# Loading only k of the first chunk by a hardware queue, q by GpSimd ahead of all, with a new order of loads and steps, in an attention-then-feed-forward kernel

## The chip, the cores and the metric

The kernel runs on one core of one Trainium2 chip. The metric is the device time of one execution in microseconds (us). The granted clock of the kernel before was 0.999 or 1.0.

## The reference, cut to what matters

```python
# q, k, v: 8 batches x 8 heads x 576 positions x 64, f32
def _attn_ref(q, k, v):                      # sliding window of 64, causal
    scores = scale * np.matmul(q, k.transpose(0, 1, 3, 2))
    mask = (rel >= 0) & (rel < 64)
    ...                                      # softmax over the window
    return np.matmul(attn, v)

def _moe_ref(x, w_gate, w_val, w_out):       # x: 4608 x 512, d_ff 1536
    g = x @ w_gate
    silu = g * (1.0 / (1.0 + np.exp(-g)))
    return silu * (x @ w_val) @ w_out
```

The 4608 tokens are worked in 36 chunks of 128. A chunk is a tile of 128 partitions by 8 heads x 64. Four chunks make one block of 512 columns for the feed-forward.

## The kernel before: what the change touches

Two lists of names make up the opening: LOADS is the order in which loads are issued, STEPS the order in which work is given to the engines. A small dependency tracker puts the waits in.

```python
    LOADS = """
    f:0:1 init kq:1 kq:2 v:0 kq:3 v:1 v:2 v:3 w:7:9 kq:5 kq:4 ... w:10:12
    """
    STEPS = """
    warm:50 ld:8 wo:0:6 B:0 ca:0:0 cd:0:1 W:4 T:0:1 T:0:0 ea:0:1 ed:0:0 TQ:1 qa:1 W:1 S:0 TK:1 ld:9 kd:1 W:1
    TQ:2 qa:2 S:1 B:2 TK:2 kd:2 A0:0 A1:0 M:1 S:2 TQ:3 N:0 B:3 TK:3 qa:3 kd:3 W:1 X:0 A0:1 xa:0 S:3 A1:1 ld:10
    A0:2 N:1 A1:2 ld:11 W:1 A0:3 N:2 A1:3 X:1 xa:1 N:3 W:1 X:2 xa:2 W:1 X:3 F:0:7:0:384 xd:3 U F:0:8 U TK:5
    TQ:5 ka:5 TQ:4 F:0:7:384:512 TK:4 ld:12 qa:4 qd:5 ka:4 U W:2 F:0:3 U S:4 S:5 F:0:6 ...
    """
```

How to read the steps: `warm:50` is 50 matmuls on zeros, `W` filler matmuls on zeros, `B` a mask product (it adds the mask to the scores' bank on TensorE), `ca`/`cd` a cast of half of chunk 0 on ScalarE or VectorE, `T` its transposes, `TQ`/`TK` the transposes of q or k of a later chunk, `qa qd ka kd` the copies of those out of PSUM (a on ScalarE, d on VectorE), `S` scores, `M` the mask on VectorE where there is no `B`, `A0`/`A1` the two halves of attention times v, `N` the normalization on VectorE, `X` the transposes of the result, `xa`/`xd` their copies, `F:c:f:t0:t1` a block of the feed-forward (weight f, columns t0 to t1), `U` its work on VectorE, `O` the last matrix product. In LOADS, `f` is chunk 0's load, `kq:n` q and k of chunk n, `v:n` its v, `w:a:b` a pair of loads of both weights.

Chunk 0's q and k come as f32 on two hardware queues and are cast; every other load comes on GpSimd's queue and is bf16 when it lands: in the trace of before, k of chunk 0 by a hardware queue is 256 KB (`ff`), a q or k chunk by GpSimd 128 KB, with no cast instruction ahead of its transposes.

```python
    def first_load(self, n, own):            # k by SP to partitions 0-63, q by ACT to 64-127
        for eng, p0, src in (("sp", 0, self.k), ("act" if own else "sp", 64, self.q)):
            ...
                a = src[b, :, s:s + L, :].rearrange("h (p j) d -> p h (j d)", j=2)
                self.g.op(eng, lambda e, d=d, a=a: e.dma_start(d, a), writes=[("ff", n, p0 + r)], dma=True)

    def init(self):
        ...                                  # identity and mask on VectorE
        dve(lambda e: e.memset(self.wz[:, 128:512], 0.0), [], ["wz2"])
        ones = self.vall[:, :].rearrange("p (i h d) -> p i h d", i=self.NV, h=H)[:, :, :, 64:80]
        dve(lambda e: e.memset(ones, 1.0), [], [("va", i) for i in range(self.NV)])
```

The column of ones beside v (only column 64 of 64 to 79 is read) makes the matmul give the softmax's sum.

The softmax here doesn't subtract the row's maximum and nothing guards it: scores larger than these inputs give would overflow.

## Time and profile before

| | before |
|---|---|
| time, median of the first 3 runs | 332.33 us (331.69 to 332.67) |
| span of the profiled run | 330.4 us |
| TensorE busy | 98% |
| first scores | 8.42 us |
| first product with v | 10.85 us |
| first normalization on VectorE | 11.97 us |
| first feed-forward matmul | 18.11 us |
| first matmul of the output product O | 71.76 us |

The instructions of the kernel before in order of time show these points. The columns are start in us, duration in us, engine (PE is TensorE, PEld its weight loads, DVE VectorE, ACT ScalarE, POOL GpSimd), line, operation, output and input, shapes, count, and in brackets the idle time before it with what ended it.

```profile
5.98 0.91 DVE L302 CAST cc<-ff 128x512 bf16<-128x512 f32 x1
...
8.42 0.45 PE L423 MATMUL ps<-qT,kT 64*64 64x128 bf16 x24 [0.41 <-DVE qT L302]
...
10.85 0.70 PE L473 MATMUL ps<-va,pt 64*64 64x65 bf16 x24
```

Read it as the path from the cast (L302) through the scores (L423) to attention times v (L473): the scores wait for a copy on VectorE.

### The profile page before, as it was taken

Reading aid. Unit: us, or ns where it says so; the run is one execution under the profiler, and the core shown is the slowest. Engines: PE = TensorE matmul, PEld = TensorE weight load, DVE = VectorE, ACT = ScalarE, POOL = GpSimd, SP = SyncE. Lnnn points to the kernel's source line nnn. Section 1 sums busy time; section 2 is a strip of 40 time slices with the busy share of each in tenths; the row PEclk is TensorE's granted clock in tenths of the full one; section 3 lists DMA queues with packets and bytes.
Section 4 is the critical chain, followed back from the end, with each engine's and each line's share of the span. In section 5 each row is a group of like instructions: output and inputs, shape, how many; then the busy total and the mean of one; then the engine's idle time right before and its main releaser. Section 6 shows DMA issues by size and latency. Waiting matters only on the chain.

```text
span 330.4 us, 8381 instructions
## 1 busy us (share of the span) xinstructions
PE 323.7 (98%) x3544; PEld 165.3 (50%) x3544; DVE 217.1 (66%) x454; ACT 137.2 (42%) x249; POOL 115.6 (35%) x144
## 2 busy tenths in 40 slices
PE   6999999999999999999999999999999999999996
PEld 4655665564455454544445454545454544444444
DVE  7569999993467858485757676767676766555520
ACT  3755466453344344343525252525343432332222
POOL 8999999965017606060706060100000000000000
DMA  9999999999999999999999999542425111100012
GB/s 133 169 170 168 165 179 155 178 139 177 197 166 173 126 148 98 158 97 160 81 177 74 182 72 163 90 111 42 122 29 131 34 63 34 63 34 32 32 65 96
DMA packets 168837, 38.70 MB, mean 117 GB/s; under 512 B 159328, under 2 KB 164320, under 8 KB 168800
## 3 DMA queue, kind: packets, MB, share of 16 engines
q0 software_dynamic: 122560, 18.62, 81.6%
q1 hardware_dynamic: 45568, 19.21, 29.6%
q8 instruction: 28, 0.46, 0.5%
q10 hardware_dynamic: 672, 0.33, 0.4%
q14 instruction: 9, 0.07, 0.1%
HBM read 37.75 MB, written 9.44 MB: 143 GB/s over the span
## 4 chain that ended last, share of the span: by engine, by line
PE 95%; DVE 4%; issue 0%; ACT 0%
PE ps L604 57%; PE ps L637 28%; PE ps L423 3%; PE ps L536 2%; PE ps L310 2%; PE ps L473 1%; DVE xb L495 1%; PE ps L667 1%; PE ps L570 1%; DVE kT L302 0%; DVE va L273 0%; DVE cc L302 0%; DVE rc L492 0%; DVE mask L267 0%; DVE pt L439 0%
## 5 line engine op out<-in xcount | busy, mean ns | idle before, releaser
L613 DVE SCALAR_TENSOR_TENSOR uu<-sig,ps 128x512 bf16<-128x512 bf16 (+3 forms) x116 | 75.1, 647 | 67.1 <-ACT sig L610 66.9
L604 PE MATMUL ps<-xT,Wg 128*128 128x512 bf16 (+3 forms) x464 | 112.3, 365 | 0.0
L604 PE MATMUL ps<-xT,Wv 128*128 128x512 bf16 (+3 forms) x464 | 112.3, 364 | 0.0
L610 ACT ACTIVATE sig<-ps 128x512 bf16<-128x512 f32 (+3 forms) x116 | 65.8, 569 | 87.5 <-PE ps L604 87.4
L637 PE MATMUL ps<-Wo,hT 128*128 128x512 bf16 x420 | 98.0, 379 | 0.2 <-issue 0.2
L615 DVE SCALAR_TENSOR_TENSOR hT<-uu,ps 128x512 bf16<-128x512 bf16 (+3 forms) x116 | 75.4, 650 | 4.0
L373 POOL DMA_DIRECT2D va<-in_v_dram x40 | 40.4, 1036 | 90.0 <-PE ps L536 87.6
L604 PEld LDWEIGHTS ps<-xT,Wv 128*128 128x128 bf16 x464 | 44.7, 98 | 49.0 <-DVE hT L615 0.3
L604 PEld LDWEIGHTS ps<-xT,Wg 128*128 128x128 bf16 x464 | 43.7, 98 | 46.1 <-DMA xT<-xb 0.3
L637 PEld LDWEIGHTS ps<-Wo,hT 128*128 128x128 bf16 x420 | 39.9, 98 | 46.9 <-issue 0.4
L649 ACT ACTIVATE ost<-ps 128x512 f32<-128x512 f32 x35 | 20.9, 597 | 66.5 <-PE ps L637 66.3
L433 ACT ACTIVATE pt<-ps 128x512 bf16<-128x512 f32 x72 | 37.7, 602 | 25.8 <-PE ps L423 25.8
L283 POOL DMA_DIRECT2D kn<-in_k_dram x39 | 40.0, 1048 | 1.6 <-DMA kn<-in_k_dram 1.6
L283 POOL DMA_DIRECT2D qn<-in_q_dram x39 | 39.9, 1042 | 1.9 <-issue 1.1
L439 DVE TENSOR_TENSOR pt<-pt,mask 128x512 bf16<-128x512 bf16 x66 | 24.3, 417 | 0.3
L558 DVE TENSOR_TENSOR xb<-ps,rp 128x448 bf16<-128x448 f32 (+1 forms) x36 | 18.5, 514 | 1.2
L555 DVE RECIPROCAL rp<-ps 128x7 f32<-128x7 f32 (+1 forms) x36 | 6.7, 187 | 15.5 <-PE ps L536 15.5
L423 PE MATMUL ps<-qT,kT 64*64 64x64 bf16 (+1 forms) x864 | 15.8, 203 | 0.6 <-DVE qT L302 0.4
L423 PEld LDWEIGHTS ps<-qT,kT 64*64 64x64 bf16 x864 | 12.3, 108 | 7.2 <-DVE hT L615 4.2
L536 PE MATMUL ps<-va,pt 64*64 64x65 bf16 x728 | 11.5, 193 | 0.1
L495 DVE TENSOR_TENSOR xb<-ps,rc 128x256 bf16<-128x256 f32 x24 | 10.2, 424 | 0.8
L379 POOL DMA_DIRECT2D Wg<-in_moe_w_gate_dram x10 | 9.8, 977 | 0.0
(51 smaller groups left out, 107.4 us busy)
## 6 DMA issues: line engine op xcount, KB each, us to landing
out_dram<-ost SPq DMA_DIRECT2D x35, 256.0 KB, 2.8
va<-in_v_dram POOLq DMA_DIRECT2D x32, 128.0 KB, 6.3
qn<-in_q_dram POOLq DMA_DIRECT2D x31, 128.0 KB, 7.0
kn<-in_k_dram POOLq DMA_DIRECT2D x31, 128.0 KB, 7.0
Wo<-in_moe_w_out_dram POOLq DMA_DIRECT2D x2, 768.0 KB, 11.4
Wg<-in_moe_w_gate_dram POOLq DMA_DIRECT2D x8, 128.0 KB, 5.0
Wv<-in_moe_w_val_dram POOLq DMA_DIRECT2D x8, 128.0 KB, 5.1
Wg<-in_moe_w_gate_dram POOLq DMA_DIRECT2D x2, 256.0 KB, 5.8
```

The lines of the kernel that those rows point to most:

```text
L283: self.g.op("pool", lambda e, d=d, a=a: e.dma_start(d, a), writes=ks, dma=True)
L373: g.op("pool", lambda e, d=d, a=a: e.dma_start(d, a), writes=ks, dma=True)
L423: r = e.matmul(sv[h][o:o + 64, c, q0:q1], self.kT[ps, c, kk:kk + 64], qT[ps, c, q0:q1], start=not biased, stop=not biased or c == 3 and kk ...
L433: g.op("act", lambda e, po=po, si=si: e.activation(po, si, ACTF.Exp, scale=SCALE), reads=[bk], writes=[pk])
L439: "dve", lambda e: e.tensor_tensor(po, po, m, ALU.mult), reads=[pk, "mask"], writes=[pk]))
L558: g.op("dve", lambda e, xo=xo, rb=rb, a=a: e.tensor_tensor(xo, a[:, :, 0:64], rb, ALU.mult), reads=[bk] + rk, writes=wk)
L604: r = e.matmul(bank[:, 0:n], W[:, kk, f * 128:f * 128 + 128], xT[:, kk, t0:t1], start=(kk == 0), stop=(kk == NK - 1))
L610: g.op("act", lambda e: e.activation(sig[:, 0:n], G[:, 0:n], ACTF.Tanh, scale=0.5), reads=[gk], writes=[("sig", i)])
L613: g.op("dve", lambda e: e.scalar_tensor_tensor(uu[:, 0:n], sig[:, 0:n], 1.0, G[:, 0:n], ALU.add, ALU.mult), reads=[("sig", i), gk], writes ...
L615: g.op("dve", lambda e: e.scalar_tensor_tensor(hT[:, f, t0:t1], uu[:, 0:n], 0.5, V[:, 0:n], ALU.mult, ALU.mult), reads=[("uu", i), vk], wr ...
L637: r = e.matmul(OB[:, :], hT[:, f, 128 * u:128 * u + 128], self.Wo[:, f, :], start=(f == 0), stop=(f == NF - 1))
L649: g.op("act", lambda e: e.activation(ost[:, :], OB[:, :], ACTF.Copy), reads=[ok], writes=[("ost", io)])
```

## The change

The intent is to shorten the path of chunk 0: half the bytes on the hardware queue, half the cast, and a smaller memset ahead of it. The two lists are new almost throughout. The diff, cut to its core:

```diff
     LOADS = """
-    f:0:1 init kq:1 kq:2 v:0 kq:3 v:1 v:2 v:3 w:7:9 kq:5 kq:4 ...
+    f:0 init q:0 kq:1 kq:2 v:1 v:0 kq:3 v:2 v:3 w:7:9 w:1:2 w:5:6 kq:4 kq:5 ...
     STEPS = """
-    warm:50 ld:8 wo:0:6 B:0 ca:0:0 cd:0:1 W:4 T:0:1 T:0:0 ea:0:1 ed:0:0 TQ:1 qa:1 W:1 S:0 ...
-    ... A0:0 A1:0 M:1 S:2 TQ:3 N:0 ... W:2 F:0:3 U S:4 S:5 F:0:6 ...
+    warm:45:64 B:0 B:1 ca:0:0 cd:0:1 T:0:1 T:0:0 ea:0:1 TQ:0 ld:8 wo:0:6 ed:0:0 qa:0 W:1 TQ:1 S:0 ...
+    ... A0:0 A0:1 A1:0 A1:1 ld:10 N:0 TQ:3 B:3 qa:3 N:1 TK:3 X:0 ka:3 xa:0 M:2 W:1 S:3 X:1 A0:2 ...
+    ... W:1 X:2 F:0:7:0:256 xd:2 U X:3 F:0:8:0:384 ... S:4 U F:0:3 kd:5 M:4 S:5 U F:0:4 ...
...
-        self.wz = sb("wz", 512)
+        self.wz = sb("wz", 128)            # fillers now read it through a broadcast
...
-        dve(lambda e: e.memset(self.wz[:, 128:512], 0.0), [], ["wz2"])
-        ones = ...[:, :, :, 64:80]
+        ones = ...[:, :, :, 64:66]
...
-    def first_load(self, n, own):
-        for eng, p0, src in (("sp", 0, self.k), ("act" if own else "sp", 64, self.q)):
+    def first_load(self, n):               # k alone, heads 0-3 and 4-7 on the partition halves
+        for u in range(2):
+            d = self.ff[n][64 * u:64 * u + 64].rearrange("p h j d -> p h (j d)")
+            a = self.k[b, 4 * u:4 * u + 4, s:s + L, :].rearrange("h (p j) d -> p h (j d)", j=2)
+            self.g.op("sp", lambda e, d=d, a=a: e.dma_start(d, a), writes=[("ff", n, u)], dma=True)
```

More of the change, by code (lines that the diff above doesn't have):

```diff
@@ L162 @@
     LOADS = """
-    f:0:1 init kq:1 kq:2 v:0 kq:3 v:1 v:2 v:3 w:7:9 kq:5 kq:4 w:3:4 w:6:7 w:4:5 v:5 w:1:2 v:4 w:9:10 w:2:3 v:6
-    w:5:6 v:7 kq:6 w:0:1 kq:7 w:10:12
+    f:0 init q:0 kq:1 kq:2 v:1 v:0 kq:3 v:2 v:3 w:7:9 w:1:2 w:5:6 kq:4 kq:5 w:3:4 w:4:5 w:6:7 v:5 w:2:3 v:6
+    v:4 w:9:10 w:0:1 kq:6 v:7 kq:7 w:10:12
     """
     STEPS = """
-    warm:50 ld:8 wo:0:6 B:0 ca:0:0 cd:0:1 W:4 T:0:1 T:0:0 ea:0:1 ed:0:0 TQ:1 qa:1 W:1 S:0 TK:1 ld:9 kd:1 W:1
-    TQ:2 qa:2 S:1 B:2 TK:2 kd:2 A0:0 A1:0 M:1 S:2 TQ:3 N:0 B:3 TK:3 qa:3 kd:3 W:1 X:0 A0:1 xa:0 S:3 A1:1 ld:10
@@ L169 @@
-    A0:2 N:1 A1:2 ld:11 W:1 A0:3 N:2 A1:3 X:1 xa:1 N:3 W:1 X:2 xa:2 W:1 X:3 F:0:7:0:384 xd:3 U F:0:8 U TK:5
-    TQ:5 ka:5 TQ:4 F:0:7:384:512 TK:4 ld:12 qa:4 qd:5 ka:4 U W:2 F:0:3 U S:4 S:5 F:0:6 M:4 F:0:4 M:5 U F:0:1 U
-    U A0:4 A0:5 A1:4 ld:13 wo:6:12 A1:5 F:0:9 N:4 N:5 X:4 F:0:2 U xa:4 X:5 U F:0:5 xd:5 F:1:1:0:128 U TQ:6
-    F:1:2:0:256 U TK:6 ld:14 qa:6 F:1:3:0:256 U F:0:0 kd:6 U U S:6 TK:7 TQ:7 F:1:0:0:256 kd:7 F:0:10 M:6 U
-    qa:7 U A0:6 S:7 A1:6 ld:15 TQ:8 TK:8 N:6 F:0:11 M:7 ka:8 qd:8 X:6 A0:7 xa:6 U S:8 A1:7 ld:16 F:1:4:0:384
@@ L174 @@
-    N:7 F:1:5:0:384 U X:7 U TQ:9 xa:7 F:1:6:0:384 M:8 qa:9 TK:9 U F:1:7 kd:9 TD:10 U A0:8 S:9 A1:8 ld:17 F:1:8
-    N:8 M:9 X:8 TQ:11 xa:8 F:1:9 U qd:11 A0:9 TK:11 U A1:9 ka:11 F:1:10 N:9 TK:12 U X:9 ka:12 TQ:12 F:1:11
-    xd:9 qd:12 TD:13 S:10 U S:12 F:1:1:128:512 M:10 F:1:0:256:512 M:12 A0:10 U S:11 A1:10 U F:1:2:256:512
-    F:1:3:256:512 N:10 F:1:4:384:512 U XD:10 F:1:5:384:512 O:0:0 U U U M:11 O:0:1 A0:11 S:13 A1:11 O:0:2 N:11
-    M:13 X:11 O:0:3 xd:11 F:1:6:384:512 U TD:14 TD:15
+    warm:45:64 B:0 B:1 ca:0:0 cd:0:1 T:0:1 T:0:0 ea:0:1 TQ:0 ld:8 wo:0:6 ed:0:0 qa:0 W:1 TQ:1 S:0 qd:1 TK:1
@@ new lines @@
+    ld:9 kd:1 W:1 TQ:2 S:1 qd:2 TK:2 kd:2 W:2 S:2 W:1 A0:0 A0:1 A1:0 A1:1 ld:10 N:0 TQ:3 B:3 qa:3 N:1 TK:3 X:0
+    ka:3 xa:0 M:2 W:1 S:3 X:1 A0:2 xd:1 A1:2 ld:11 N:2 W:1 A0:3 A1:3 N:3 W:1 X:2 F:0:7:0:256 xd:2 U X:3
+    F:0:8:0:384 xd:3 F:0:1 U U F:0:5 U TK:4 TQ:4 ld:12 ka:4 TQ:5 F:0:7:256:512 qd:4 TK:5 qa:5 F:0:8:384:512 U
+    S:4 U F:0:3 kd:5 M:4 S:5 U F:0:4 M:5 U F:0:6 U F:0:2 U A0:4 A0:5 A1:4 ld:13 wo:6:12 A1:5 F:0:9 N:4 N:5 X:4
+    F:0:0 U xa:4 X:5 U TK:6 xa:5 TQ:6 ld:14 F:1:0:0:128 ka:6 U F:1:1:0:256 qa:6 TQ:7 U F:1:2:0:256 qd:7 S:6
@@ new lines @@
+    TK:7 U F:1:3:0:256 kd:7 F:0:10 M:6 U U A0:6 S:7 A1:6 ld:15 TQ:8 TK:8 N:6 F:0:11 M:7 ka:8 qd:8 X:6 A0:7
+    xa:6 S:8 U A1:7 ld:16 F:1:4:0:384 N:7 F:1:5:0:384 U X:7 U TQ:9 xa:7 F:1:6:0:384 M:8 qa:9 TK:9 U F:1:7 kd:9
+    TD:10 U A0:8 S:9 A1:8 ld:17 F:1:8 N:8 M:9 X:8 TQ:11 xa:8 F:1:9 U qd:11 A0:9 TK:11 U A1:9 ka:11 F:1:10 N:9
+    TK:12 U X:9 ka:12 TQ:12 F:1:11 xd:9 qd:12 TD:13 S:10 U S:12 F:1:0:128:512 M:10 F:1:1:256:512 M:12 A0:10 U
+    S:11 A1:10 U F:1:2:256:512 F:1:3:256:512 N:10 F:1:4:384:512 U XD:10 F:1:5:384:512 O:0:0 U U U M:11 O:0:1
@@ L179 @@
+    A0:11 S:13 A1:11 O:0:2 N:11 M:13 X:11 O:0:3 xd:11 F:1:6:384:512 U TD:14 TD:15
     """
@@ L209, in alloc @@
         self.qT = [self.qa[:, :, r, :] for r in range(self.NZ)]
-        pairs = lambda t: t[:, :].rearrange("p (h j d) -> p h j d", h=H, j=2)
-        self.ff = [pairs(t) for t in ring("ff", self.NI, H * 128, F32)]
-        self.cc = [t[:, :].rearrange("p (j h d) -> p j h d", j=2, h=H) for t in ring("cc", self.NI, H * 128)]
+        pairs = lambda t: t[:, :].rearrange("p (h j d) -> p h j d", h=H // 2, j=2)
+        self.ff = [pairs(t) for t in ring("ff", self.NI, H * 64, F32)]
+        self.cc = [t[:, :].rearrange("p (j h d) -> p j h d", j=2, h=H // 2) for t in ring("cc", self.NI, H * 64)]
         self.one, self.fi, self.df = [sb(x, 128, F32) for x in ("one", "fi", "df")]
@@ L270, in init, with load_qk @@
         dve(lambda e: e.memset(self.kT[:, :, 0:64], 0.0), [], [("kT", -1, j) for j in range(2)])
-        dve(lambda e: e.memset(self.wz[:, 128:512], 0.0), [], ["wz2"])
-        ones = self.vall[:, :].rearrange("p (i h d) -> p i h d", i=self.NV, h=H)[:, :, :, 64:80]
+        ones = self.vall[:, :].rearrange("p (i h d) -> p i h d", i=self.NV, h=H)[:, :, :, 64:66]
         dve(lambda e: e.memset(ones, 1.0), [], [("va", i) for i in range(self.NV)])
-    def load_qk(self, n):
+    def load_qk(self, n, which="qk"):
         i = n % self.NQ
-        for dst, src, nm in ((self.qn[i], self.q, "qn"), (self.kn[i], self.k, "kn")):
+        for w in which:
+            dst, src, nm = (self.qn[i], self.q, "qn") if w == "q" else (self.kn[i], self.k, "kn")
             parts = list(self.segs(128 * n, 128))
@@ L283, in load_qk @@
                 self.g.op("pool", lambda e, d=d, a=a: e.dma_start(d, a), writes=ks, dma=True)
-    def first_load(self, n, own):
-        for eng, p0, src in (("sp", 0, self.k), ("act" if own else "sp", 64, self.q)):
-            parts = list(self.segs(128 * n, 128))
-            for r, b, s, L in parts:
-                d = self.ff[n][p0 + r // 2:p0 + (r + L) // 2].rearrange("p h j d -> p h (j d)")
-                a = src[b, :, s:s + L, :].rearrange("h (p j) d -> p h (j d)", j=2)
-                self.g.op(eng, lambda e, d=d, a=a: e.dma_start(d, a), writes=[("ff", n, p0 + r)], dma=True)
+    def first_load(self, n):
+        (_, b, s, L), = self.segs(128 * n, 128)
+        for u in range(2):
+            d = self.ff[n][64 * u:64 * u + 64].rearrange("p h j d -> p h (j d)")
+            a = self.k[b, 4 * u:4 * u + 4, s:s + L, :].rearrange("h (p j) d -> p h (j d)", j=2)
+            self.g.op("sp", lambda e, d=d, a=a: e.dma_start(d, a), writes=[("ff", n, u)], dma=True)
     def cast(self, n, half, eng):
-        hs = slice(4 * half, 4 * half + 4)
+        hs = slice(2 * half, 2 * half + 2)
         d = self.cc[n][:, :, hs].rearrange("p j h d -> p h j d")
-        self.move(eng, d, self.ff[n][:, hs], [("ff", n, p) for p in (0, 64)], [("cc", n, half)])
+        self.move(eng, d, self.ff[n][:, hs], [("ff", n, u) for u in (0, 1)], [("cc", n, half)])
     def move(self, eng, d, a, rk, wk):
@@ L316, in first_T @@
     def first_T(self, n, half):
-        job = [self.cc[n][:, j, 2 * c:2 * c + 2, :] for c in (2 * half, 2 * half + 1) for j in range(2)]
+        job = [self.cc[n][:, j, 2 * half:2 * half + 2, :] for j in range(2)]
         self.transposes(("f", n, half), job, [("cc", n, half)])
@@ L321, in first_ev @@
         tb, bk = self.tb["f", n, half]
-        cs = slice(2 * half, 2 * half + 2)
-        ta = tb.rearrange("p (c j) (w t) -> p w c t j", j=2, w=2)
-        kd, qd = self.kT[:, cs, 64 + 128 * n:192 + 128 * n], self.qT[n][:, cs]
-        for w, (d, key) in enumerate(((kd, ("kT", n, half)), (qd, ("qT", n, half)))):
-            self.move(eng, d.rearrange("p c (t j) -> p c t j", j=2), ta[:, w], [bk], [key])
+        d = self.kT[:, half:4:2, 64 + 128 * n:192 + 128 * n].rearrange("p u (t j) -> p u t j", j=2)
+        self.move(eng, d, tb[:, 0:2].rearrange("p j (u t) -> p u t j", u=2), [bk], [("kT", n, half)])
         self.done(bk)
@@ L341, in ev, with warm @@
         self.done(bk)
-    def warm(self, count):
+    def warm(self, count, cols):
         bank, bk = self.ps[7], ("ps", 7)
+        a = self.wz[:, 0:128].unsqueeze(1).to_broadcast([128, cols // 128, 128]) if cols > 128 else self.wz[:, 0:cols]
         def pe(e):
             for _ in range(count):
-                r = e.matmul(bank[:, 0:64], self.wz[:, 0:128], self.wz[:, 0:64], start=True, stop=True)
+                r = e.matmul(bank[:, 0:cols], self.wz[:, 0:128], a, start=True, stop=True)
             return r
@@ L353, in fill @@
     def fill(self, count):
+        a = self.wz[:, :].unsqueeze(1).to_broadcast([128, 4, 128])
         j = min(self.pool, key=lambda i: self.pool[i])
@@ L358, in pe @@
             for _ in range(count):
-                r = e.matmul(bank[:, :], self.wz[:, 0:128], self.wz[:, :], start=True, stop=True)
+                r = e.matmul(bank[:, :], self.wz[:, :], a, start=True, stop=True)
             return r
-        self.g.op("pe", pe, reads=["wz", "wz2"], writes=[bk])
+        self.g.op("pe", pe, reads=["wz"], writes=[bk])
     def load_v(self, n):
@@ L685, in build @@
         acts = {
-            "f": self.first_load, "init": self.init, "v": self.load_v, "w": W, "kq": self.load_qk,
+            "f": self.first_load, "init": self.init, "v": self.load_v, "w": W, "kq": self.load_qk, "q": lambda n: self.load_qk(n, "q"), "k": lambda n: self.load_qk(n, "k"),
             "wo": self.load_wo, "ld": load,
```

## The prediction

> **What bounds the kernel now.** I read the page first: the busy rows, the slices, the chain that ended last.
>
> ```profile
> PE 323.7 (98%) x3544; PEld 165.3 (50%) x3544; DVE 217.1 (66%) x454; ACT 137.2 (42%) x249; POOL 115.6 (35%) x144
> ...
> PE   6999999999999999999999999999999999999996
> ...
> PE 95%; DVE 4%; issue 0%; ACT 0%
> ...
> ff<-in_k_dram SPq DMA_DIRECT2D x1, 256.0 KB, 5.1
> ff<-in_q_dram ACTq DMA_DIRECT2D x1, 256.0 KB, 3.8
> ```
>
> TensorE is 9 in every slice but the first and the last, and the chain is 95% TensorE. No later wait is worth attacking: only useless TensorE time can go, and that is in the opening. So I read the chain in order of time over the first 60 us:
>
> ```profile
> 4.83 1.10 DVE va L273
> 5.93 0.05 issue
> 5.98 0.93 DVE cc L302
> 6.91 0.05 issue
> 6.96 0.63 PE ps L310 x8
> ...
> 8.42 0.45 PE ps L423 x17
> ...
> 13.60 0.25 PE ps L473 x16
> ...
> 17.88 0.40 PE ps L570 x4
> 18.28 3.03 PE ps L604 x16
> ...
> 22.64 0.43 PE ps L359 x2
> ```
>
> L423 is a score matmul, L473 attention times v, L604 the feed-forward, L359 filler on zeros. The feed-forward starts at 18.28 us; from there TensorE is unbroken, and 0.43 us of filler at 22.64 is the only waste. The time is therefore "start of the feed-forward, less useful work done before it, plus filler and gaps after it". The instructions in order of time show what the opening waits for:
>
> ```profile
> 4.87 0.90 POOL L373 DMA_DIRECT2D va<-in_v_dram  x1
> ...
> 10.06 0.83 POOL L379 DMA_DIRECT2D Wg<-in_moe_w_gate_dram  x1
> 10.80 0.83 POOL L379 DMA_DIRECT2D Wv<-in_moe_w_val_dram  x1
> ...
> 14.45 0.18 DVE L492 RECIPROCAL rc<-ps 128x4 f32<-128x4 f32 x1 [0.97 <-PE ps L473]
> ```
>
> GpSimd issues loads back to back from 1.25 us, one per 0.87 us for a q, k or v chunk and 0.74 for a weight. Asked one by one, the first lands 5.1 us after issue, the next six after 4.6, the first weight pair after 5.4 and 5.9. So the v of chunk 0 lands at 4.87 + 4.6 = 9.5 and that weight pair at 15.5 and 16.7: before they are used (10.85, 18.11). Compute, not loads, sets this opening; VectorE normalizes chunk 0 from 12.0 to 13.2, idles 0.97, then chunks 1 to 3 until 17.83.
>
> [...] chunk 0's q and k arrive as f32 and need 0.63 us of ScalarE and 0.91 of VectorE to cast, while a q from GpSimd needs none. [...] q and k were both issued at 0.74 on two queues, and landed 3.8 and 5.1 us later. [...] 64 elements took 112 ns, 192 took 218, 1280 took 1125, i.e. about 0.83 ns each plus 60. [...] the granted clock reads 1.00 throughout: the two mask matmuls (L403) at 4.33 took 609 ns each, the fillers at 5.15 380.
>
> **The change part by part.**
>
> 1. The ones memset shrinks from 8x10x16 = 1280 to 160 elements: 0.06 + 160 x 0.83 = 0.2 us instead of 1.13. The 0.22 us zero memset (wz2) goes. VectorE's setup ends near 4.65 instead of 5.93.
> 2. The hardware load is halved: k alone, in two pieces on one queue. The q load, equally large and first through, landed at 0.74 + 3.8 = 4.5; I take that for both pieces of k, against 5.84 now. The casts halve: 0.46 us VectorE, 0.38 ScalarE (the row of 128x256 evictions). Casts end near 5.15, not 6.91.
> 3. But two mask products, B:0 and B:1, now stand ahead of the transposes: four cold matmuls of about 0.41 us spacing from 4.33, so TensorE is free near 5.7. Of the 1.75 us gained on VectorE some 0.5 is lost here.
> 4. q of chunk 0 comes as GpSimd's first load: with its first-load latency, 1.25 + 5.1 = 6.35; with less hardware traffic beside it, perhaps 6.0. Then TQ:0 0.2, eviction qa:0 0.60 on ScalarE. q of chunk 1, second in the queue, lands at 2.25 + 4.6 = 6.85, and its transpose stands before S:0. Scores of chunk 0 run at about 7.1 to 7.3 instead of 8.42: 1.2 us gained.
> 5. Every GpSimd load behind q slides by one slot, 0.87 us, and v of chunk 0, now behind v of chunk 1, by two: issue 6.60, landing 11.2. k of chunk 2 lands at 9.5, so S:2 can run at 10.35 (before 11.44). A0:0 then stands at 11.2, not 10.85: the 1.2 us are spent waiting for v.
> 6. With A0:0, A0:1, A1:0, A1:1 in one block (56 small matmuls, 0.86 us; 52 took 0.79 later), the norm of chunk 0 starts at 12.0, the same as before, but chunk 1's follows without the 0.97 us idle. VectorE from 12.03: two norms of 1.09 = 14.2; mask of chunk 2 0.72 = 14.9; xT copy 0.42, about 0.2 waited on either side of it; norm of chunk 2 to 16.8. X:2 takes 0.25, so the feed-forward starts at 17.05 with F:0:7:0:256, needing only chunks 0 and 1. Its first weight lands at 10.93 + 5.4 = 16.3, the second at 11.67 + 5.9 = 17.6 against a need at 17.5. It takes half of a 1.73 us block, 0.87; X:3 0.22; then F:0:8:0:384 waits for norm 3 (17.9) and its xT copy (18.3) and starts at about 18.35.
>
> Sum: at 18.35 the new kernel has 0.87 us of feed-forward behind it; the old one at 18.28 none. 0.87 - 0.07 = 0.80 us. The two fillers at 22.64 are not in the new list: + 0.43. Splitting one more 512 block costs TensorE nothing: 384 + 128 columns take 1.30 + 0.45 against 1.73. So **1.2 us** are gained at about 23 us.
>
> 7. What is given back: the load queue is 0.87 us later and TensorE 1.2 earlier, so every load loses 2.1 us of slack. Walking both lists on with the landing times above, most weights still come 0.3 to 1 us ahead. The exception is the last pair, w:10:12: issued at 35.21 and 35.96, landing after 6.3 and 6.9 us, i.e. 41.5 and 42.9, used at 43.25 and 44.11. New: landing 42.4 and 43.7, wanted at 42.1 and 42.9, so some 0.4 to 0.8 us of waiting. Against that, the old kernel's 0.13 us wait for the q eviction at 45.3 goes. Net gain 0.5 to 1.2; I take 1.1, leaning to the upper end as the list has been searched again with these waits in it. 332.33 - 1.1 = **331.2 us**.
>
> After 46 us nothing differs, and the loads run ahead (landing 10 to 18 us after issue, kept back by buffers), so whatever lead is left reaches the end.
>
> **Rivals.**
>
> A: *load-bound opening*. q ahead of all makes q, k and v of the next chunks set the pace, and the opening loses what the cast gained. For: point 5, and loads already back to back. Against: in the old kernel each load had 0.7 to 2 us of slack. If landings come 0.5 us later than I assume, the start is no earlier than before and the time is 332.3 to 332.8.
>
> B: *the whole early lead survives*. If k lands at 4.2, v of chunk 0 sooner than 11.2, and F:0:7 starts near 16.3, the lead is 2 us and more, and 330 us results. For: each step from S:0 to S:2 is 1.1 to 1.3 us earlier. Against: v of chunk 0 was moved two slots back, and the norms, 4 x 1.09 us on VectorE, cannot overlap.
>
> C: *hidden anyway*. TensorE waits at w:10:12, or at another load between 20 and 45 us, until its lead is gone: only the removed filler's worth or nothing remains, 332.0 to 332.3.
>
> D: *the clock*. 45 warm-up matmuls rather than 50, then a gap until 4.33: if the array stays at half speed through B:0 and B:1 and the transposes, 0.3 us go, for 331.5.
>
> **Range and chances.** The lead at 23 us is 1.2, uncertain by 0.5 either way; the giving back is 0 to 0.8; the runs of before spread by 1.0 us, so a median of three may be off by 0.3. Eight in ten: 330.0 to 332.4. A 2% change is 6.6 us, more than a third of the whole opening of 18 us, of which a good half is needed work: 0.01 faster, 0.98 same, 0.01 slower.
>
> **What would show it.** Right: setup of VectorE over by 4.7; k landing within 4 us of issue; first scores at 7.1 to 7.3; TensorE's first v product waiting for the v load at about 11.2; no VectorE idle between norms 0 and 1; first feed-forward at 17.0; no filler after 18 us; TensorE waits on Wg or Wv near 42 us. Wrong: a first feed-forward before 16.5 or after 17.8, a TensorE wait of more than 1 us between 18 and 45, or any difference after 60 us, where I expect a mere shift.

The sum: 0.80 and 0.43 make the 1.2 us, less 0.4 to 0.8 given back, plus 0.13; it took 1.1 and came to 331.2 us. The 64, 192 and 1280 elements are those of three memsets on VectorE, and 0.83 ns each plus 60 is an estimate from their times. The "cold" TensorE and its "half speed" are what the trace of before shows at a granted clock of 1.0: its two mask products of 128x512 start 0.40 us apart at 4.33 us, and 0.22 apart at 12.05. "Perhaps 6.0" for q's landing was a guess; that first load of GpSimd took 5.1 us in before and 4.9 in after.

## The result

| | before | after |
|---|---|---|
| median of 4 runs | 332.28 us (331.69 to 332.67) | 332.10 us (332.03 to 332.19) |
| ratio | | 0.9996, 95% interval 0.9979 to 1.0014 |
| span of the profiled run | 330.4 us | 329.9 us |
| first transposes of chunk 0 | 6.96 us | 6.03 us |
| first scores | 8.42 us | 7.86 us |
| first product with v | 10.85 us | 11.47 us |
| first normalization | 11.97 us | 12.22 us |
| first feed-forward matmul | 18.11 us | 17.48 us |

A ratio here is the mean time of one kernel's runs over that of the other's of the same rounds, so it is not quite the ratio of the medians quoted beside it. The time lies in the predicted range; but of the 1.1 us that were expected to be gained, 0.2 show in the medians, and none in a second set of runs (below). The question is therefore where 1.1 us went.

The page of the kernel after, its busy row:

```profile
PE 320.5 (97%) x3505; PEld 166.2 (50%) x3543; DVE 217.0 (66%) x457; ACT 136.0 (41%) x247; POOL 116.5 (35%) x145
```

The slices are the old ones, but for the first, which moved from 6 to 7. TensorE's count needs care: 3505 matmuls stand against 3543 weight loads, so 38 matmul records are missing from this trace, and the gaps of 0.16 us in its chain are put down to them (at the output product, L635, 405 matmuls stand against 420 weight loads, and 2.1 us of such gaps against 0.2 in before). They are called "issue": time in which the engine waited for nothing that the profile shows. What follows uses starts of instructions that are there, and the weight loads where a matmul is missing.

The instructions of the kernel after in order of time, columns as above:

```profile
4.39 0.19 DVE L272 MEMSET va<- 128x160 bf16 x1
...
5.67 0.29 DVE L301 CAST cc<-ff 128x256 bf16<-128x256 f32 x1 [1.09 <-DMA ff<-in_k_dram]
...
6.03 0.62 PE L309 MATMUL ps<-ident,cc 128*128 128x128 bf16 x4
...
7.86 0.64 PE L421 MATMUL ps<-qT,kT 64*64 64x128 bf16 x24
...
11.47 0.75 PEld L471 LDWEIGHTS ps<-va,pt 64*64 64x64 bf16 x56 [0.23 <-DMA va<-in_v_dram]
...
16.00 0.18 DVE L490 RECIPROCAL rc<-ps 128x4 f32<-128x4 f32 x1 [0.43 <-PE ps L471]
...
18.09 0.33 PEld L602 LDWEIGHTS ps<-xT,Wv 128*128 128x128 bf16 x4 [0.29 <-DMA Wv<-in_moe_w_val_dram]
```

Two of the brackets now name a load on GpSimd's queue, which they did not before: v of chunk 0 at 11.47 and the second weight at 18.09. The scores are 0.56 us earlier than before, the product with v that follows them 0.62 us later. The third bracket, 0.43 us of VectorE at 16.00, is the normalization chain waiting for chunk 2's product with v.

The chain that ended last is the work that set the end of the run, each piece waiting for the one before. That of the kernel after, in order of time (start, duration, what):

```profile
4.33 1.89 PE ps L401 x4
6.22 0.85 PE ps L309 x8
...
17.65 0.44 PE ps L602 x4
...
18.93 1.30 PE ps L602 x8
...
25.89 0.38 PE ps L421 x17
...
28.10 0.38 PE ps L421 x17
```

The four mask products (L401) hold TensorE until 6.2: they start 0.40 to 0.43 us apart, where two of the same shape at 12.72 start 0.22 apart. The eight transposes behind them (L309) take 0.85 us, where eight took 0.44 in the kernel before. The feed-forward's first half block starts at 17.65 in the chain and the next block at 18.93. The last two lines are the scores of chunks 4 and 5, apart from each other here. In the chain of the kernel before they are one burst:

```profile
24.80 0.63 PE ps L423 x34
```

**Counting the lead.** The lead is how far the new kernel is ahead of the old one at the same amount of work. At 18.93 the new kernel has half a block done, worth 0.87 us (half of 1.73); the old one starts its block at 18.28 in its chain. The opening's lead is thus 0.87 - (18.93 - 18.28) = 0.22 us. The removed fillers give 0.43. The two score bursts cost 0.38 + 0.38 and lengthen the block behind each from 1.73 to 1.83, together 0.96, against 0.63 + 0.10 = 0.73 before: 0.23 lost. That makes 0.42. The direct count agrees: the product with v of chunk 4 starts at 33.69 against 30.65, with two more feed-forward blocks of 1.73 done before it, so 30.65 + 3.46 - 33.69 = 0.42. At the first weight load of the output product 0.24 is left (71.51 against 71.75). The net loss of 0.18 lies in two places where a weight load waits for the feed-forward's own product hT on VectorE (L613), 0.25 us at 39.86 and 0.24 here, less a wait near 45 us that only the kernel before has:

```profile
46.14 0.55 PEld L602 LDWEIGHTS ps<-xT,Wg 128*128 128x128 bf16 x4 [0.24 <-DVE hT L613]
```

TensorE's own line there, at 46.37, names a normalization, but the first of its four matmuls is one of the missing records. At 72.95 the kernel before has a stall in its profiled run (shown with e6 below), which takes the lead to 0.56; from 90 us to the end it is 0.4.

### The profile page after: what moved, and what is told of

Read it like the earlier page. It is cut to its first block, busy times and chain, and to the rows that moved or that the text cites. A ratio compares the mean times of both kernels' runs of the same rounds, so it can differ in the third digit from the quotient of the medians.

```text
span 329.9 us, 8342 instructions
## 1 busy us (share of the span) xinstructions
PE 320.5 (97%) x3505; PEld 166.2 (50%) x3543; DVE 217.0 (66%) x457; ACT 136.0 (41%) x247; POOL 116.5 (35%) x145
## 4 chain that ended last, share of the span: by engine, by line
PE 95%; DVE 2%; issue 1%
PE ps L602 56%; PE ps L635 27%; PE ps L421 3%; PE ps L534 2%; PE ps L309 2%; PE ps L471 2%; PE ps L665 1%; PE ps L568 1%; PE ps L401 1%; DVE xb L493 1%; PE ps L357 0%; DVE kT L301 0%; DVE mask L267 0%; DVE hT L613 0%; DVE pt L437 0%
## 5 line engine op out<-in xcount | busy, mean ns | idle before, releaser
L602 PE MATMUL ps<-xT,Wg 128*128 128x512 bf16 (+3 forms) x447 | 108.1, 362 | 2.0 <-issue 0.6
L635 PE MATMUL ps<-Wo,hT 128*128 128x512 bf16 x405 | 94.6, 379 | 2.2 <-issue 2.1
L613 DVE SCALAR_TENSOR_TENSOR hT<-uu,ps 128x512 bf16<-128x512 bf16 (+3 forms) x117 | 75.6, 646 | 4.0
L371 POOL DMA_DIRECT2D va<-in_v_dram x40 | 39.7, 1026 | 89.4 <-PE ps L534 87.3
L635 PEld LDWEIGHTS ps<-Wo,hT 128*128 128x128 bf16 x420 | 39.9, 98 | 46.6
L283 POOL DMA_DIRECT2D qn<-in_q_dram x40 | 40.7, 1037 | 2.6 <-issue 1.8
L534 PEld LDWEIGHTS ps<-va,pt 64*64 64x64 bf16 x728 | 9.4, 108 | 0.6 <-DVE hT L613 0.4
```

Of the source, the lines that this page charges most:

```text
L283: self.g.op("pool", lambda e, d=d, a=a: e.dma_start(d, a), writes=ks, dma=True)
L371: g.op("pool", lambda e, d=d, a=a: e.dma_start(d, a), writes=ks, dma=True)
L534: r = e.matmul(bb[b][0][ws, 65 * sl:65 * sl + 65], self.pt[(n + j) % self.NP][ks, h, ws], vv[ks, h, 0:65], start=m == q[0], stop=m == q[-1])
L602: r = e.matmul(bank[:, 0:n], W[:, kk, f * 128:f * 128 + 128], xT[:, kk, t0:t1], start=(kk == 0), stop=(kk == NK - 1))
L613: g.op("dve", lambda e: e.scalar_tensor_tensor(hT[:, f, t0:t1], uu[:, 0:n], 0.5, V[:, 0:n], ALU.mult, ALU.mult), reads=[("uu", i), vk], wr ...
L635: r = e.matmul(OB[:, :], hT[:, f, 128 * u:128 * u + 128], self.Wo[:, f, :], start=(f == 0), stop=(f == NF - 1))
```

## The experiments

The chosen theory, **LOADS**, says that the order and rate of GpSimd's load queue set the opening: q put ahead of all pushes v and the first weights back, and what the scores gain is waited for again at v. The rivals: **CLOCK**, TensorE's half pace until about 8.7 us spends the gain (in the kernel after, transposes start 106 ns apart from 6.0 us on and 56 from 9.0 on, at a granted clock of 1.0; the texts call it half clock or half speed); **NORM**, the normalizations on VectorE and the steps around them set the feed-forward's start whatever v does; **PATH** and **HIDDEN**, what q's way and the smaller memset are worth by themselves, or whether they are hidden anyway. Two came up on the way: **SHARED RINGS**, q's packets hold back k's, and **INSTRUCTION REFILL**, the guess that a stall of TensorE with no cause in the profile goes with a transfer of the queue of kind "instruction" that ended shortly before (1.34 to 1.49 us in three traces, below). All kernels gave correct results.

### e1: the kernel after, once more

No edit.

> The changed kernel once more, unaltered, to see how well its milestones repeat and to narrow the ratio. All theories: time 332.1 +/- 0.2, ratio to the kernel before 0.998 to 1.001; TensorE's first feed-forward matmul at 17.5 us, first score matmul of chunk 0 at 7.86, the four mask matmuls (B:0, B:1) at 600 ns each (half clock). If the slow clock before 8.4 us was chance, the first 8 transposes take 220 ns each this time and the scores come at 7.3.

Measured: 332.27 us (332.17 to 332.41, 5 runs) against 332.02 (331.47 to 332.65, 11 runs), ratio 1.0007, 95% 0.9995 to 1.0019. The scores are at 7.86 again, v at 11.55, the feed-forward at 17.87, the product with v of chunk 4 at 34.01: a lead of 0.1 us there, where the first trace had 0.42. At the second feed-forward block it is 0.02 (19.13 in its chain) and not 0.22, and at the output product it is gone. So the lead itself varies by some 0.3 us from one profiled run to the next, and in this set of runs none of it is in the time.

### e2: 60 warm-ups in place of 45

```diff
-    warm:45:64 B:0 B:1
+    warm:60:64 B:0 B:1
```

> 60 warm-up matmuls instead of 45, which closes the gap ahead of the mask matmuls at 4.33. Theory CLOCK (the array stayed at half clock until 8.4 because of that gap, and this cost the lead): the transposes of chunk 0 take 220 ns instead of 380, the first scores come at 7.3 to 7.4 instead of 7.86, the first feed-forward at 17.0, the time falls by 0.4 to 0.6 us. Theory LOADS (v of chunk 0, landing at 11.3, and the first Wv, landing at 18.07, set the opening): the scores come 0.5 us earlier, but the first product with v starts at 11.35 to 11.5 as now, the feed-forward at 17.3 to 17.5, and the time falls by less than 0.2 us.

Measured: 332.29 us (332.20 to 332.74), the same time as e1. The instructions of e2 in order of time:

```profile
7.34 0.45 PE L421 MATMUL ps<-qT,kT 64*64 64x128 bf16 x24 [0.25 <-ACT qT L299]
...
11.94 0.88 PE L471 MATMUL ps<-va,pt 64*64 64x65 bf16 x56 [1.09 <-DMA va<-in_v_dram]
```

TensorE's pace is repaired from 6.1 us on (the mask products still start about 0.43 us apart): the eight transposes start 55 ns apart instead of 106, and the scores come 0.52 us sooner. In the profiled runs with 45 warm-ups and 0.73 us of idle behind them the slow pace lasted until 8.3 us or later (after, e1, e3, e4); with 50 and some 0.46 us it ended between 4.3 and 7.0 (before, e5, e6, e9, e11); the granted clock read 1.0 in all of them. But TensorE then stands 1.09 us for v, and the feed-forward is no earlier (17.95). The slow pace is real and worth nothing here (332.29 us against 332.27); LOADS holds.

### e3: one more load behind q

```diff
-    f:0 init q:0 kq:1
+    f:0 init q:0 v:9 kq:1
```

> One more load of 128 KB (a v chunk that is loaded again later) right behind q of chunk 0 on the GpSimd queue: doubles the suspected cost, every later load lands 0.85 us later. Theory LOADS: first product with v at about 12.3 instead of 11.47, first feed-forward about 0.8 us later (18.3), further waits on weights up to 43 us, time up by 0.8 to 1.2 us. Theory CLOCK or NORM (VectorE's norms and masks set the start of the feed-forward, loads have slack): time up by less than 0.3 us.

Measured: 333.14 us (332.48 to 334.51), ratio 1.0038 (1.0013 to 1.0062).

```profile
12.99 0.95 PE L471 MATMUL ps<-va,pt 64*64 64x65 bf16 x56 [1.21 <-DMA va<-in_v_dram]
```

This line of the instructions in order of time is to be read against 11.55 in e1. The feed-forward starts at 19.00 (17.87 in e1), and from 90 us on the trace is 1.2 us behind that of e1. The medians differ by 0.87. One slot of the load queue, 0.87 us, costs about its own length. That is LOADS by its own dose.

### e4: the new lists with the old way of q

The kernel before, with its own first load, cast and memset, and the new lists in it:

```diff
     (against the new lists)
-    f:0 init q:0 kq:1 ...
+    f:0:1 init kq:1 ...
-    warm:45:64 ... ea:0:1 TQ:0 ld:8 wo:0:6 ed:0:0 qa:0 W:1 ...
+    warm:45 ... ea:0:1 ld:8 wo:0:6 ed:0:0 W:1 ...
```

> Undoes one part: q and k of chunk 0 both come by the two hardware queues as in the kernel before (with its memsets and casts), but the searched list of loads and of steps of the changed kernel stays. Loads on the GpSimd queue then land 0.85 us earlier, the scores of chunk 0 come later (8.4 or more, because the casts end at 6.9). Theory LOADS: v of chunk 0 lands at 10.4, the first product with v starts when the scores allow, 11.6 to 11.9; the feed-forward starts at 17.4 to 17.8 and no Wv wait follows; time as the changed kernel within 0.3 us: the q path is worth nothing because what it gains at the scores it gives back at v. Theory CAST (the removed casts and memset are worth their 1 us): time 0.6 to 1.0 us above the changed kernel.

Measured: 332.83 us, but in two groups (331.73 and 331.88, then 332.81 to 333.52), ratio 1.0018 (1.0000 to 1.0035). In its trace the scores come at 8.84, v at 12.88, the feed-forward at 18.89, which is 1.0 us behind e1 and, in the part after 90 us, 0.8 behind before. So with these lists the new way of q, with the smaller cast and memset that go with it, looks worth something (PATH: about 0.6 us in the medians, 1.0 in the traces), and these lists on the old way look worse than the old lists on the old way. The times do not settle it: two of the six runs are quicker than every run of e1, and the two intervals overlap. And e4's TensorE ran at half its pace until after 9 us (a filler of 128x512 took 0.63 us at 9.82; before's took 0.38 at 7.63), so part of its lateness is that pace. As the traces have it, the change is a pair: a quicker path, and an order of loads that gives about as much back.

### e5: the kernel before without its two fillers at 22.6 us

```diff
-    ... ka:4 U W:2 F:0:3 ...
+    ... ka:4 U F:0:3 ...
```

> One part alone, on the kernel before: only the two fillers that it runs at 22.64 us (0.43 us of TensorE) are taken out. The prediction's term (they are pure waste, worth 0.43 us): time of the kernel before less 0.4, block of F:0:3 starting at 22.65 instead of 23.08 and everything behind it 0.43 earlier. Rival (they fill a wait: weights, PSUM banks or evictions bind there): less than 0.15 us.

Measured: 331.79 us (331.43 to 332.39, 6 runs) against 332.16 (331.77 to 333.55, 11 runs), ratio 0.9986 (0.9969 to 1.0003). The product with v of chunk 4 comes 0.43 us sooner (30.22 against 30.65), and the output product 0.42 (71.34). The filler's 0.43 us is whole TensorE time and reaches the end; the medians show 0.37. This one deletion gives as much as the traces show of the whole change.

### e6: the kernel before with the small memset alone

```diff
-        ones = ...[:, :, :, 64:80]
+        ones = ...[:, :, :, 64:66]
```

> One part alone, on the kernel before: only the ones memset is cut from 1280 to 160 elements. VectorE's setup then ends at about 5.0 instead of 5.93, but the f32 q and k of chunk 0 land at 5.8 (k), so the cast can start only 0.1 us earlier. Theory HIDDEN: time within 0.15 us of the kernel before. Theory CAST (VectorE's setup was the bound of the opening): the cast and the scores 0.9 us earlier and the time down by 0.5 us or more.

Measured: 332.37 us (332.22 to 333.76), ratio 1.0010 (0.9987 to 1.0032): no difference. Its trace holds two surprises. The instructions in order of time, first in the opening and then at 72 us:

```profile
5.93 0.43 DVE L302 CAST cc<-ff 128x512 bf16<-128x512 f32 x1 [1.14 <-DMA ff<-in_k_dram]
...
7.88 0.45 PE L423 MATMUL ps<-qT,kT 64*64 64x128 bf16 x24 [0.41 <-DVE qT L302]
...
74.53 4.48 PE L637 MATMUL ps<-Wo,hT 128*128 128x512 bf16 x20 [1.76 <-issue]
```

The cast starts only 0.05 us sooner than before, since it waits for k's load as the prediction thought (HIDDEN). Yet it takes 0.43 us instead of 0.91, and the scores come at 7.88 — as early as with the whole change. This is not the memset's doing: e9, e11 and e12 have the same small memset, and their scores come at 8.42 or 8.43. The cast goes with the load that GpSimd is issuing meanwhile, in before (the first line, beside the cast at 5.98) and in e6 (the second):

```profile
5.73 0.91 POOL L283 DMA_DIRECT2D qn<-in_q_dram  x1
```

```profile
5.73 1.11 POOL L283 DMA_DIRECT2D qn<-in_q_dram  x1
```

In before, e4, e5, e9, e11 and e12 the cast starts anywhere from 5.98 to 6.29 and ends at 6.90 in all six, 0.25 us after GpSimd's instruction, which runs to 6.65. The half-size cast starts from 5.10 to 5.47 in e1, e2, e3, e7 and e8 and ends at 5.89 or 5.90, 0.11 after one that runs to 5.78; in e10, where the loads are moved, it ends at 5.00, 0.11 after 4.89. In e6 the cast ended at 6.36, and GpSimd's instruction is the one that took 0.2 us longer (1.11 against 0.91). Only the first trace of after (5.67 to 5.97) fits neither. So in twelve of these fourteen traces the end of VectorE's cast lies 0.11 or 0.25 us after GpSimd's load instruction, and how early the cast can start matters little.

Nor does this early start last: the lead of 0.40 us at the product with v of chunk 4 (30.25) is 0.15 at 46.04, behind a wait of 0.25 us for k of a later chunk, and 0.02 at the output product.

The other surprise is the stall of 1.76 us with "issue" as its cause: TensorE waited for nothing that the profile shows. The kernel before has a small one at the same instruction (0.53 us from start to start where its neighbours have 0.22, so 0.32 us lost):

```profile
72.95 4.48 PE L637 MATMUL ps<-Wo,hT 128*128 128x512 bf16 x20 [0.16 <-issue]
```

The profiled run of e6 is its 333.76; its other three took 332.22 to 332.47. So one execution in four here was 1.3 to 1.5 us longer, and its trace has a stall of that size.

### e7 and e8: v of chunk 0 ahead of v of chunk 1, with the steps to fit

Both start from e2. In e7 the loads are swapped and chunk 0's product and normalization stand before chunk 1's; e8 also moves chunk 2's mask ahead.

```diff
-    ... kq:2 v:1 v:0 kq:3 ...
+    ... kq:2 v:0 v:1 kq:3 ...
-    ... A0:0 A0:1 A1:0 A1:1 ld:10 N:0 ...
+    ... A0:0 A1:0 N:0 A0:1 A1:1 ld:10 ...
     (e8 only)
-    ... qa:3 N:1 TK:3 X:0 ka:3 xa:0 M:2 W:1 S:3 ...
+    ... qa:3 M:2 N:1 TK:3 X:0 ka:3 xa:0 W:1 S:3 ...
```

> The changed kernel with 60 warm-up matmuls (as in the run above), v of chunk 0 loaded ahead of v of chunk 1, and the products with v of chunk 0 and its norm ahead of those of chunk 1. Theory LOADS (v of chunk 0 in the seventh slot is what ate the lead that the earlier scores gave): first product with v at 10.5 to 11 instead of 11.94, norm 0 starting 0.9 us earlier than in the run with 60 warm-ups alone, first feed-forward at 17.3 to 17.5; time down by 0.4 to 0.7 us against that run, i.e. 331.6 to 331.9. Theory NORM (the order of norms and mask on VectorE binds, not v): norm 0 starts earlier but the feed-forward starts within 0.2 us of 18.1, and the time stays at 332.2.

> As the run before this one, and the mask of chunk 2 goes ahead of norm 1 on VectorE, so that the products with v of chunk 2 are done while norm 1 runs. Theory NORM: VectorE's idle stretch ahead of norm 2 (0.43 to 0.49 us in the changed kernel and the run with 60 warm-ups) goes and the feed-forward starts 0.2 to 0.4 us earlier than in the run before this one, if the second weight (landing at 17.6 to 18.1) allows; the time falls by another 0.2 to 0.3 us. Theory LOADS alone: no further gain, since the first feed-forward then waits for Wv.

Measured: e7 332.22 us (331.65 to 333.58), ratio 0.9998 (0.9979 to 1.0018); e8 332.12 us (331.74 to 332.51), ratio 0.9993 (0.9978 to 1.0009). The instructions of e7 in order of time:

```profile
10.78 0.70 PE L471 MATMUL ps<-va,pt 64*64 64x65 bf16 x24
...
12.23 0.71 PE L471 MATMUL ps<-va,pt 64*64 64x65 bf16 x32 [0.75 <-DMA va<-in_v_dram]
```

Chunk 0's product comes 1.16 us sooner than in e2, and now chunk 1's waits for its own v, 0.75 us. The feed-forward starts at 17.58, 0.37 sooner than in e2; the output product, 0.27. Moving the mask (e8) gained nothing more: 17.73 and 71.83. So one wait for a load is replaced by the next one, as LOADS has it, and the times do not resolve what is left. NORM, as far as the mask's place goes, is not supported.

### e9: the old loads of q and k, with the norms placed as in the new lists

The kernel before with the small memset of e6 and these lists:

```diff
-    f:0:1 init kq:1 kq:2 v:0 kq:3 v:1 v:2 ...
+    f:0:1 init kq:1 kq:2 v:0 v:1 kq:3 v:2 ...
-    ... S:2 TQ:3 N:0 B:3 TK:3 qa:3 kd:3 W:1 X:0 A0:1 xa:0 S:3 A1:1 ld:10 A0:2 N:1 A1:2 ...
+    ... S:2 N:0 A0:1 A1:1 ld:10 N:1 TQ:3 B:3 qa:3 TK:3 X:0 ka:3 xa:0 W:1 S:3 X:1 xa:1 A0:2 A1:2 ...
-    ... X:3 F:0:7:0:384 xd:3 U F:0:8 ... F:0:7:384:512 ... ka:4 U W:2 F:0:3 ...
+    ... F:0:7:0:256 X:3 xd:3 U F:0:8 ... F:0:7:256:512 ... ka:4 U F:0:3 ...
```

> A candidate from the kernel before, with its own path for q and k of chunk 0 (both by hardware queues): small ones memset, the two fillers at 22.64 gone, v of chunk 1 loaded ahead of q and k of chunk 3, and the products with v and the norm of chunk 1 ahead of chunk 3's work, so that VectorE runs the four norms without the 0.97 us idle. Theory LOADS AND NORMS (the start of the feed-forward is set by when v arrives and by VectorE's chain of norms; the q path has little to do with it): norm 1 right after norm 0, first feed-forward at 16.7 to 17.1 instead of 18.1, waits on weights of up to 0.5 us after it, lead of 1.0 to 1.6 us at 72 us, time 330.7 to 331.3. Theory PATH (q by GpSimd is what makes an earlier opening possible): no better than the changed kernel, 331.9 or more.

Measured: 331.74 us (331.22 to 332.07, 5 runs) against 331.93 (331.65 to 332.44, 9 runs), ratio 0.9992 (0.9978 to 1.0005). The instructions in order of time:

```profile
15.97 0.18 DVE L481 RECIPROCAL rc<-ps 128x4 f32<-128x4 f32 x1 [1.73 <-PE ps L462]
...
19.23 1.04 PE L593 MATMUL ps<-xT,Wg 128*128 128x512 bf16 x4 [0.52 <-DVE xT L291]
```

Norms 0 and 1 run back to back and the feed-forward begins at 17.45, the earliest of all; but VectorE then idles 1.73 us before norm 2, and the second block waits 0.52 us for its input. The lead at the output product is 0.17 (71.59 against 71.76), less than e5's 0.42 although e9 contains e5's edit. The gap was moved, not removed.

### e10: q held back until k has landed

The kernel after, with q's load made to wait for the setup tile df, which VectorE writes from 2.39 us on. It is issued at 2.99 us instead of 1.25.

```diff
-     self.g.op("pool", lambda e, d=d, a=a: e.dma_start(d, a), writes=ks, dma=True)
+     self.g.op("pool", lambda e, d=d, a=a: e.dma_start(d, a), reads=["df"] if w == "q" and n == 0 else [], writes=ks, dma=True)
```

> The changed kernel, but GpSimd's first load (q of chunk 0) waits until VectorE has written the difference matrix at 2.68 us: issue at about 2.75 instead of 1.25, every load 1.5 us later, and k of chunk 0 has the rings to itself until about 4.7. Theory SHARED RINGS (k's second half landed at 5.3 to 5.6 and not at the predicted 4.5 because q's packets ran beside it): k's second half lands 2.8 to 3.1 us after its issue, at 4.3 to 4.6. Rival (the second transfer of a queue is just slow, 3.5 to 4.1 us): it lands at 5.2 or later. Theory LOADS: first product with v at 12.9 to 13.4, first feed-forward at 18.9 to 19.4, time up by 1.0 to 1.6 us; if loads had slack, up by less than 0.5.

Measured: 333.77 us (333.49 and 334.05, 2 runs, one with a granted clock of 0.995), ratio 1.0054 (1.0036 to 1.0073). Time from issue to landing of the two halves of k (minimum, median, maximum of two), first in the kernel after, then in e10; each line is the last of the answer for the tile ff:

```profile
DMA to landing us min/median/max: 2.7/3.4/4.1
```

```profile
DMA to landing us min/median/max: 2.8/2.8/2.8
```

In the trace of the kernel after the first packets of q move at 3.0 us and the second half of k is among them; in e10 they begin at 4.7, when k is through. So SHARED RINGS is supported, by one trace of each kind: the second half of k was 1.3 us slower with GpSimd's loads, q first of all, beside it. It did not matter: the transposes come at 5.73 instead of 6.03, as the mask products hold TensorE, and every load issued 1.5 to 1.7 us later puts v at 13.73 and the feed-forward at 19.74. This is a second dose of LOADS, twice that of e3, and the time follows: 1.5 us over e1.

### e11: e9 with chunk 2's v and product earlier

```diff
     (from e9)
-    ... v:2 v:3 w:7:9 ...
+    ... v:2 w:7:9 v:3 ...
-    ... ka:3 xa:0 W:1 S:3 X:1 xa:1 A0:2 A1:2 ld:11 N:2 W:1 A0:3 A1:3 N:3 W:1 X:2 xa:2 F:0:7:0:256 X:3 xd:3 U F:0:8 U ...
+    ... ka:3 X:0 xa:0 A0:2 A1:2 ld:11 N:2 W:1 S:3 X:1 xd:1 W:1 X:2 xa:2 A0:3 A1:3 N:3 F:0:7:0:256 U F:0:8:0:384 X:3 xd:3 U ...
```

> The candidate of the run before with two orders mended that its trace shows to bind: the products with v of chunk 2 go ahead of chunk 3's scores (VectorE idled 1.73 us ahead of norm 2 there), the first weights are loaded ahead of v of chunk 3 (they landed at 15.8 and 17.0), and the first two feed-forward blocks are cut so that TensorE does not wait 0.52 us for xT of chunk 3. Theory LOADS AND NORMS: norm 2 follows norm 1 with less than 0.5 us between, the feed-forward starts at 16.2 to 16.9 and TensorE has no wait over 0.2 us after it up to 23 us; lead at 72 us of 0.9 to 1.5 us over the kernel before, time 330.8 to 331.3, ratio 0.996 to 0.998. Theory PATH: no better than 331.7. Rival LOADS LATER: the opening is earlier by 1 us or more but TensorE waits for weights between 20 and 45 us and the lead at 72 us is under 0.6.

Measured: 332.94 us (332.38 to 333.39, 5 runs) against 332.27 (9 runs), ratio 1.0018 (1.0005 to 1.0032). It should have been a little faster, and it was slower. The chain that ended last, of the slowest of the five runs:

```profile
68.58 2.86 PE ps L593 x31
71.44 1.76 issue
73.20 0.23 PE ps L593
```

Until there the kernel is ahead of before: 0.43 us at the product with v of chunk 4 (30.22). The stall at 71.44 takes more than all of it.

### The stall: what the three traces have in common

The trace also holds the packets of each transfer. A queue of the kind "instruction" (q8 on the page: 28 transfers, 0.46 MB) moves throughout. Counting the instructions of TensorE in order, the stalled one has the same number in each of the three traces, and a transfer of that queue had just ended:

| trace | TensorE instruction | transfer ended | instruction started | after |
|---|---|---|---|---|
| before | 2242nd | 71.46 | 72.95 | 1.49 |
| e6 | 2242nd | 73.19 | 74.53 | 1.34 |
| e11 | 2242nd | 71.78 | 73.20 | 1.42 |

In e11 that instruction is another piece of work than in before (a feed-forward matmul, not an output one): the three stalls share the place in the program, not the work. 28 transfers against 7,190 TensorE instructions make one per 257. If INSTRUCTION REFILL is right, a shift of the program by some instructions moves the work that is hit.

### e12: e11's steps, with 15 more warm-ups ahead

```diff
     (from e11)
-    ... v:2 w:7:9 v:3 ...
+    ... v:2 v:3 w:7:9 ...
-    warm:50 ...
+    warm:65 ...
```

> The candidate of the run before with two edits: v of chunk 3 loaded ahead of the first weights again (TensorE waited 0.81 us for it), and 15 more warm-up matmuls, which move TensorE's program so that the place where it stood 1.76 us near 72 us (at the 1095th weight load; the kernel before and the run with the small memset alone stood at the 1097th, for 0.16 and 1.76 us, each just after a late transfer of the queue of kind instruction) falls elsewhere; the three runs with 15 more warm-ups had no such wait. Theory INSTRUCTION REFILL: no wait of that kind over 0.3 us near 72, the lead that the opening has at 30 us reaches the end. Theory LOADS AND NORMS: products with v of chunk 3 at 16.5 to 16.7, lead at 30 us of 0.8 to 1.2 us. Both right: 331.0 to 331.5, ratio 0.996 to 0.998. If the wait near 72 has to do with the earlier arrival itself (loads of Wo, PSUM), it stays and the time is 332.5 to 333.

Measured: 332.98 us (332.51 to 334.56, 6 runs) against 332.22 (10 runs), ratio 1.0040 (1.0018 to 1.0061). The two longest runs (334.20 and 334.56) are those with a granted clock of 0.995; the other four, 332.51 to 333.11, are still 0.7 us above before in the mean. In the trace the stall at 72 us is gone. Two others stand in the opening, in the instructions in order of time:

```profile
13.36 0.25 PE L462 MATMUL ps<-va,pt 64*64 64x65 bf16 x7 [0.58 <-issue]
...
19.76 0.27 PE L593 MATMUL ps<-xT,Wv 128*128 128x256 bf16 x1 [0.83 <-issue]
```

They are TensorE's 450th and 706th instructions; the transfers ended at 11.74 and 18.24 us, 1.62 and 1.52 us before. 450, 706 and 2242 lie 256 and six times 256 apart. I then looked at every 256th instruction from 450 to 2242 (eight in each) in the traces of before and the twelve experiments; that of after, with records missing, can't be counted so. In before the 2242nd is the one that comes soonest after a transfer, the other seven 2.2 to 9.2 us after the last one. In none of the 104 did the instruction start less than 1.27 us after the last transfer had ended, and the "issue" stalls of e6, e11 and e12 all lie between 1.34 and 1.62. In e2 and e7 the 706th instruction came 1.4 us after its transfer with no stall of note.

So that the stalls go with these transfers is supported from three sides (the spacing of 256, the transfers' ends, the moved stall); that TensorE waits for the transfer itself is the author's reading, which no trace shows as a wait. The hoped gain failed: the lead at 30 us that e11 had is eaten in the opening. Two things stay open. Why a transfer of these ends so shortly before its place was not tried; what the traces show is only that the 16 transfer engines are 90% busy or more at these times. And that the spread of before's runs (331.47 to 333.55 over all rounds) comes from these stalls is argued from e6, where one run has both, and not shown: unprofiled runs leave no trace.

## Why the prediction was right or wrong

The class and the range were right: the change moves an opening of 18 us of a kernel that TensorE fills from there on. But the range of 330.0 to 332.4 also holds before's own 332.28, so that it was met says nothing for the mechanism; that is luck of its width. After 90 us every trace is a shift of before's, within some 0.1 us. "After 60" was predicted, and between 72 and 90 us it fails: the stalls move the lead there (0.24, 0.56, 0.4). The point value was 0.9 us too low. In part that is the prediction's own sum: 1.2, less 0.4 to 0.8, and 0.13 make 0.5 to 0.9, and it took 1.1. By its own steps:

| term of the sum | predicted | in the profiled run |
|---|---|---|
| opening, at the second feed-forward block | +0.80 | +0.22 |
| fillers at 22.6 us removed | +0.43 | +0.43 |
| waits for the last weights at 42 us | -0.4 to -0.8 | 0 |
| scores of chunks 4 and 5 set apart | not seen | -0.23 |
| waits from 34 to 47 us, one of before's removed | +0.13 | about -0.18 |
| lead at the output product | 0.5 to 1.2 | 0.24 |

The last column is one trace of the kernel; in e1's the first line is +0.02 and the last is nothing.

1. **Memset**: right, 0.19 us, and VectorE's setup ends at 4.58. That its removal would only bring the cast forward to k's landing was right too; that the cast ends 0.11 us after GpSimd's load instruction in six of the seven traces of this load, and takes 0.29 to 0.79 us, was left out.
2. **Landing of k**: wrong. 4.5 us was taken for both halves; the second landed at 5.6 in the first trace and near 5.3 in e1 to e3. The step left q's packets out (e10). The casts were to end near 5.15; VectorE's ended at 5.97, and at 5.89 in e1 to e3, with GpSimd's load instruction (e6). The next step hid this.
3. **The mask products**: right in kind, too small in size. They hold TensorE not to 5.7 but to 6.0: all four start 0.40 to 0.43 us apart and the transposes behind them 106 ns, twice the later 0.22 us and 56 ns. That was rival D, sized at 0.3 us; it is 0.5 at the scores (e2) and nothing in the time.
4. **Scores at 7.1 to 7.3**: 7.86, from that pace (7.34 in e2). q's landing, the disputed part, was right (6.1 against 6.0 to 6.35).
5. **v of chunk 0 is what the gain is spent on**: right, and the core of the matter. 11.2 was predicted, 11.47 measured, with the load in the bracket. e3 and e10 show that the opening gets later with this queue by about the same amount. The other direction is not shown: e7 brings v of chunk 0 sooner, and the times show no gain.
6. **From the norms to the feed-forward**: this is the step that failed in size, +0.80 us predicted and +0.22 measured. Norms 0 and 1 do run back to back, and the wait around the copy before norm 2 is as sized (0.43 us at 16.00, against twice 0.2). But norm 0 is 0.2 us late (12.22 against 12.03), norm 2 is 0.3 late (16.00 against 15.7), and norm 3 ends 0.4 late (18.28 against 17.9). The first half block starts at 17.48 against 17.05, and inside it the second weight lands at 18.07, 6.4 us after issue and not 5.9, for 0.29 us of waiting. The next block starts at 18.76 against 18.35: 0.41 of the 0.80 us are gone. Another 0.17 was a misreading: the working held its own start of 18.35 against 18.28 of the old chain, where a piece begins when the one before has ended; the first matmul of that block starts at 18.11.
7. **What is given back**: right in amount, wrong in place. No wait for a weight is to be seen at 42 us: the last pair landed at 41.74 and 43.09, and its weight loads begin at 42.88 and 43.64. What was given back went to the two score bursts and to the waits for hT. The step looked for loads and not at the cost of interrupting the feed-forward twice.

Of the rivals, A (a load-bound opening) came nearest by its mechanism, and it should have had the most weight; its time, 332.3 to 332.8, is a little too long. B is refuted by v at 11.47 and the feed-forward at 17.5. C has the right time, 332.0 to 332.3, and the wrong reason: the lead was not eaten by a weight, it never got large.

No version tried beats both kernels beyond its interval. The nearest is the deletion of two filler matmuls (e5, 0.9986, 0.9969 to 1.0003).

## What to carry to other kernels

When loads are issued back to back on one queue, putting one of them first costs every later one a slot (0.87 us here, and e3's extra slot cost 0.87 us of time), so work out the landing of the last load that the opening needs before counting the gain of the first. Along a chain across two engines small delays add up, and starts have to be compared with starts; the 0.6 us that the working missed here were half of the gain it expected. And where a trace shows TensorE standing for no cause (0.16 to 1.76 us here), count its instructions and look at the instruction queue's transfers (1.3 to 1.6 us before the stalled instruction here) before giving the difference to the change.
